# Two zero regions of dv: copied from memory by GpSimd in transfers of 4, 2, 2 and 8 rows, with one zero store issued earlier

## The chip, the cores and the metric

The kernel runs on one core of one Trainium2 chip. The metric is the device time in microseconds (us), from start to end of the program. Before the change its median over three runs is 283.13 us (282.75 to 283.57). The profiled execution took 283.0 us, of which the profile shows a span of 281.0 us; all times of events below are counted from the start of that span.

A core has five engines with instruction streams of their own: PE (matrix products), DVE and ACT (elementwise work and moving results out of the accumulators), POOL or GpSimd, and SP or SyncE, which computes nothing and here issues nearly all transfers. Transfers between memory (DRAM) and the on-chip buffer (SBUF) are carried out by 16 DMA engines, and a transfer of 128 rows is dealt out over all of them. GpSimd and ACT can issue transfers too, through queues of their own, onto the same 16 engines.

## The reference

The reference is one decoding step of a small transformer block and the gradients of all its inputs. Four sequences, one new token each, width 512. Attention has 32 query heads on 8 key/value heads of size 128, over a cache of 4096 positions of which only the last W = 1024 are used:

```python
W = min(4096, max(256, Sk // 4))                                # 1024 of 4096
q = (x @ wq).reshape(B, Sq, Hq, Dh).transpose(0, 2, 1, 3)
k = jnp.repeat(k_cache[:, :, Sk - W:, :], rep, axis=1)
v = jnp.repeat(v_cache[:, :, Sk - W:, :], rep, axis=1)
p = softmax(einsum("bhqd,bhkd->bhqk", q, k) * Dh ** -0.5)
A = einsum("bhqk,bhkd->bhqd", p, v).transpose(0, 2, 1, 3).reshape(B, Sq, Hq * Dh) @ wo
ffn = (gelu(xn @ w_gate) * (xn @ w_up)) @ w_down                # xn = layernorm(x), x of A
out = x + A(xn) + ffn(xn)
outputs: out, d x, d k_cache, d v_cache, d wq, d wo, d w_gate, d w_up, d w_down
```

What matters here: the gradients of the two caches have the caches' full shape, (4, 8, 4096, 128) in bf16, 33.6 MB each. Only the last 1024 positions of each head hold computed values. The first K0 = 3072 positions are zero and have to be written all the same: 25 MB in each, 50 MB in all, of the 81 MB that the kernel writes.

## The kernel before

Outputs are called out_0 to out_8; out_2 is dk, out_3 is dv, out_4 the gradient of wq (dwq), out_5 that of wo (dwo), out_6 to out_8 those of the feed-forward weights.

First comes the feed-forward part (lines 552 to 715), then a loop over NT = 4 groups t of two key/value heads each (lines 725 to 753). In a group the scores are formed from the keys, softmax follows, the same with the values, and then the gradients. Work that can wait (the products for dv, dk, dwo and dwq, and moving them to staging tiles) is put into a queue of small pieces, `bg`, and `tick(n)` takes n pieces from it between the steps of the main work. So the pieces for dwo, dk and dwq of group t are done during group t+1, and those of the last group at the end (line 754).

Every finished staging tile is stored by SyncE through `store` (line 100), which sets out that output stores write disjoint parts and need not wait for each other. Stores of computed data are of kind "rest", those of zeros of kind "zeros".

The zeros come from one SBUF tile, `ztile` (128 rows of 6144 bf16 values, 12,288 bytes each), cleared by GpSimd at the start (line 167). The list `zlist` (line 159) holds 32 regions: for each sequence b and each pair of heads g, one of out_2 and one of out_3, in turn. `zero(n)` (line 161) takes the next n regions from its front and stores each with one SyncE transfer of 1.5 MB: 128 rows of 12,288 bytes, eight for each DMA engine.

Where the zero stores stand is written out by hand: three at the start, one behind some of the feed-forward stores, one behind every dv and dk store (line 490), a few by themselves in the first group, four in the last group after the steps on the values (`zero(4)`, line 734), and whatever is left at the end (line 755). SyncE issues in program order, so a zero store also stands ahead of all stores that follow it. By the end two regions are left, the last two of sequence 3.

GpSimd issues six loads of weights (`load_w`, line 120). Its last instruction in group 3 is the product o_s inside `odq(t, 0)` (line 463); after that it has nothing to do. The change touches `zero`'s list, `piece_q` (the dwq pieces, line 513, with the store at line 524), and the main loop.

## Time and profile before

| what | before |
|---|---|
| time, median of 3 | 283.13 us |
| span of the profile | 281.0 us |
| PE, DVE, ACT, POOL busy | 72%, 58%, 42%, 14% of the span |
| moved by DMA | 112.12 MB, mean 399 GB/s |
| read from, written to memory | 30.68 MB, 81.01 MB |
| queue of SyncE | 103.56 MB, 89.6% of the 16 engines' span |
| queue of GpSimd | 6.29 MB, 5.6% |
| last SyncE stores issued | 263.25 us (two zero stores) |
| zero stores | 32 of 1536 KB, median 18.1 us from issue to landing |

In the windows and the page, "DMA share" is the mean busy share of the 16 DMA engines: 1.00 is all of them, 0.06 is one. Its value can be a little over 1, since packets overlap at their ends. A transfer "lands" engine by engine: each of the 16 engines reports its own share as done, and the transfer is complete when the last has reported. An issue on SyncE (SPq in the views) is the instruction that starts a transfer; the transfer itself runs later, behind those already queued.

### The profile page before, as it was taken

How to read it: one execution, taken by the hardware profiler on the slowest of the kernel's cores; microseconds unless marked ns; L12 is line 12 of the kernel's file. 1: busy time of each engine (PE TensorE's matmuls, PEld its weight loads, DVE VectorE, ACT ScalarE, POOL GpSimd, SP SyncE). 2: the span in 40 equal slices, each digit the busy share in tenths (PEclk: the TensorE clock that was granted, in tenths of full speed). 3: DMA queues.
4: the chain of work that ended last, by engine and by line, in shares of the span. 5: the costliest groups of instructions: out<-in, count | busy, mean ns of one | idle time of the engine just before them, and what ended most of it. 6: DMA issues, size and time to landing. Idle time of an engine off the chain costs nothing.

```text
span 281.0 us, 6867 instructions
## 1 busy us (share of the span) xinstructions
PE 203.1 (72%) x2972; PEld 138.8 (49%) x2972; DVE 164.1 (58%) x313; ACT 117.8 (42%) x219; POOL 40.1 (14%) x40
## 2 busy tenths in 40 slices
PE   0276699959789889998999299898999599390000
PEld 0265476735456665566775156677556484140000
DVE  7946646645776655577666067767677728386000
ACT  2030386635035418764448056443866038370000
POOL 8600000007002150002250000223000400000000
PEclk9999589986999999999999969999999979977555
DMA  7999999999999999999999999999999999999990
GB/s 264 393 375 431 431 426 417 425 419 424 369 395 424 422 420 420 426 415 422 419 417 411 412 424 423 431 383 398 385 368 415 387 432 410 425 429 422 398 422 30
DMA packets 19565, 112.12 MB, mean 399 GB/s; under 512 B 1664, under 2 KB 4496, under 8 KB 11088
## 3 DMA queue, kind: packets, MB, share of 16 engines
q1 hardware_dynamic: 17744, 103.56, 89.6%
q0 software_dynamic: 1632, 6.29, 5.6%
q10 hardware_dynamic: 160, 1.84, 1.9%
q8 instruction: 23, 0.38, 0.5%
q14 instruction: 6, 0.05, 0.0%
HBM read 30.68 MB, written 81.01 MB: 397 GB/s over the span
## 4 chain that ended last, share of the span: by engine, by line
PE 47%; DMA 22%; DVE 16%; ACT 4%; issue 2%; SPq 0%; DVEq 0%; ACTq 0%
DMA out_dram<-stg_dv 13%; PE T_ps L279 8%; PE kv_ps L484 7%; DMA wd_sb<-in_B_w_down_dram 6%; PE S_ps L345 5%; PE od_ps L450 5%; DMA out_dram<-osb_g 4%; DVE T_sb L98 3%; DVE dS_s L367 2%; PE wdT_ps L279 2%; PE dwq_ps L520 2%; PE acc_ps L256 2%; PE dwd_ps L660 2%; DVE P_s L367 2%; PE wgT_ps L279 2%
## 5 line engine op out<-in xcount | busy, mean ns | idle before, releaser
L98 DVE COPY T_sb<-T_ps 128x1024 bf16<-128x1024 bf16 x64 | 44.1, 688 | 26.7 <-PE T_ps L279 26.5
L97 ACT CAST stg_dk<-kv_ps 128x512 bf16<-128x512 f32 x52 | 29.2, 588 | 31.2 <-PE kv_ps L484 12.4
L97 ACT CAST stg_dv<-kv_ps 128x512 bf16<-128x512 f32 x51 | 28.1, 588 | 24.9 <-PE kv_ps L484 24.3
L484 PE MATMUL kv_ps<-qmr,dS_s 128*128 128x512 bf16 x64 | 23.9, 414 | 11.3 <-ACT stg_dk L97 10.6
L463 POOL TENSOR_TENSOR o_s<-od_r,msk_r 128x512 bf16<-128x512 bf16 x8 | 9.1, 1157 | 110.2 <-DVE od_r L455 80.9
L484 PE MATMUL kv_ps<-domr,P_s 128*128 128x512 bf16 x64 | 21.3, 382 | 0.0
L279 PE MATMUL T_ps<-ident,vb 128*128 128x128 bf16 x256 | 20.3, 225 | 0.4 <-DVE T_sb L98 0.4
L279 PE MATMUL T_ps<-ident,kb 128*128 128x128 bf16 x256 | 20.4, 225 | 0.0
L279 PEld LDWEIGHTS <-kb 128*128 128x128 bf16 x256 | 17.5, 101 | 4.5 <-issue 1.3
L279 PEld LDWEIGHTS <-vb 128*128 128x128 bf16 x256 | 17.2, 101 | 5.0 <-issue 3.2
L97 ACT CAST osb_q<-dwq_ps 128x512 bf16<-128x512 f32 x25 | 14.6, 587 | 8.3 <-PE dwq_ps L520 7.4
L329 POOL TENSOR_TENSOR domr<-r,msk 128x1024 bf16<-128x1024 bf16 x4 | 7.6, 1892 | 71.2 <-DVE r L326 65.1
L97 ACT CAST osb_g<-dwg_ps 128x512 bf16<-128x512 f32 (+1 forms) x25 | 12.3, 544 | 12.3 <-PE dwg_ps L673 6.3
L97 ACT CAST osb_o<-dwo_ps 128x512 bf16<-128x512 f32 x24 | 13.9, 586 | 4.5 <-PE dwo_ps L505 2.9
L98 DVE CAST stg_dk<-kv_ps 128x512 bf16<-128x512 f32 x12 | 8.0, 688 | 12.0 <-DMA out_dram<-stg_dv 11.2
L98 DVE COPY wgT<-wgT_ps 128x1024 bf16<-128x1024 bf16 x14 | 9.6, 686 | 6.8 <-PE wgT_ps L279 6.8
L345 PE MATMUL S_ps<-T_sb,qm 128*32 128x256 bf16 x128 | 12.7, 387 | 0.6 <-DVE T_sb L98 0.5
L345 PE MATMUL S_ps<-T_sb,dom 128*32 128x256 bf16 x128 | 12.7, 388 | 0.1
L505 PE MATMUL dwo_ps<-dyr,o_s 128*128 128x512 bf16 x32 | 12.4, 413 | 0.3 <-ACT stg_dk L97 0.2
L98 DVE COPY woT<-woT_ps 128x1024 bf16<-128x1024 bf16 x16 | 11.0, 686 | 2.7 <-PE woT_ps L279 2.3
L484 PEld LDWEIGHTS <-dS_s 128*128 128x128 bf16 x64 | 6.2, 101 | 12.2 <-issue 11.1
L520 PE MATMUL dwq_ps<-od_r,xnm 128*128 128x256 bf16 x64 | 11.6, 274 | 0.3 <-ACT osb_q L97 0.2
(188 smaller groups left out, 385.0 us busy)
## 6 DMA issues: line engine op xcount, KB each, us to landing
out_dram<-ztile SPq DMA_DIRECT2D x32, 1536.0 KB, 18.1
kb<-in_A_k_cache_dram SPq DMA_DIRECT2D x8, 1024.0 KB, 17.4
vb<-in_A_v_cache_dram SPq DMA_DIRECT2D x8, 1024.0 KB, 20.7
out_dram<-stg_dv SPq DMA_DIRECT2D x8, 1024.0 KB, 13.0
out_dram<-stg_dk SPq DMA_DIRECT2D x8, 1024.0 KB, 20.8
out_dram<-osb_o SPq DMA_DIRECT2D x8, 512.0 KB, 17.4
out_dram<-osb_q SPq DMA_DIRECT2D x8, 512.0 KB, 13.8
out_dram<-osb_g SPq DMA_DIRECT2D x8, 448.0 KB, 14.3
```

The source lines that it names most:

```text
L97: return nc.scalar.copy(out=out, in_=in_)
L98: return nc.vector.tensor_copy(out=out, in_=in_)
L256: nc.tensor.matmul(ps[:, c, :], lhsT=lf(c), rhs=rhs, start=(k == 0), stop=(k == len(terms) - 1))
L279: nc.tensor.transpose(ps[:, i, :], a, ident[:])
L329: nc.gpsimd.tensor_tensor(out=mr[:].rearrange("p g q d -> p (g q) d"), in0=r4[:, k, :].unsqueeze(1).broadcast_to([P, SL, Dh]), in1=msk[:]. ...
L345: nc.tensor.matmul(ps[b * RB:(b + 1) * RB, :], lhsT=zt[:, b * GP + g, c0:c0 + RB], rhs=T_sb[:].rearrange("p (x b) -> p b x", b=B)[:, b, :] ...
L367: nc.vector.scalar_tensor_tensor(out=out[:], in0=src[:].unsqueeze(2).broadcast_to([P, WQ, B]), scalar=rr[:, 0:1], in1=mskb[:].unsqueeze(1) ...
L450: nc.tensor.matmul(od_ps[g * 32:g * 32 + B * rep, k, g, :], lhsT=cols[:, jj, g * NQ + q, :], rhs=blks[(t, g)][:, j, :], start=(j == 0), st ...
L463: nc.gpsimd.tensor_tensor(out=o_s[:, g], in0=rows[:, g].unsqueeze(1).broadcast_to([P, rep, Dh]), in1=msk_r[:].unsqueeze(2).broadcast_to([P ...
L484: nc.tensor.matmul(mps[:].rearrange("p q d -> p (q d)"), lhsT=src[:, j * P:(j + 1) * P], rhs=mr[:, g].rearrange("p q d -> p (q d)"), start ...
L505: nc.tensor.matmul(mps[:], lhsT=o_s[:, g].rearrange("p r d -> p (r d)")[:, i:rep * Dh:rep], rhs=dyr[:], start=True, stop=True)
L520: nc.tensor.matmul(mps[:, i].rearrange("p g d -> p (g d)"), lhsT=xnm[:, i2 * 2 + i, c * P:(c + 1) * P], rhs=dq_r[:].rearrange("p g d -> p ...
```

## The change

Three edits:

1. A function `zero_14` takes the last two out_3 regions (sequence 3, heads 4 to 7, one block of four heads x 3072 positions) out of `zlist`. The first 14/16 of each head's positions are written by three GpSimd transfers of 4, 2 and 8 rows (a row is 192 positions of each of the four heads), which copy zeros from out_2[0], where they have been stored long before. Between the first and the second of these stands a short transfer of two rows of 4 KB from `ztile`. It writes 32 positions of one head. The last 2/16 of each head, less those 32 positions, are left to four SyncE stores from `ztile`, of 16 rows each, that are returned as a list and issued at the very end.
2. `zero_14` is called in the last group after `odq(t, 0)`, that is, behind the product o_s on GpSimd.
3. One zero store is issued earlier, behind the last dwq store of group 1 (the second group); and the last group's `zero(4)` becomes `zero(2)`. With the two regions gone, one full zero store is left for the end, followed by the four small ones.

The purpose of 1 is to let a part of the zeros be written by chosen DMA engines rather than by all 16 alike: 4 + 2 + 8 rows go to fourteen of them[...]. All zeros are still written, each once.

```diff
+    def zero_14():
+        last = [z for z in zlist if z[0] is out_3][-2:]
+        for z in last:
+            zlist.remove(z)
+        b, g = last[0][1:]
+        assert last[1][1:] == (b, g + ZR)
+        dst = out_3[b, g:g + 2 * ZR]
+        NH, KR = 4, K0 // 16
+        k0 = 14 * KR
+
+        def rest(eng, n, h, k0, w):
+            src = ztile[0:8 * n - 7:8] if n < 16 else ztile[0:n]
+            store(eng, dst[h, k0:k0 + n * w, :].rearrange("(m j) d -> m (j d)", m=n), src[:, 0:w * Dh], "zeros")
+
+        r0 = 0
+        for n in (4, 0, 2, 8):
+            if not n:
+                rest(nc.gpsimd, 2, 0, k0, 16)
+                continue
+            s_, d_ = (x[0:NH, r0 * KR:(r0 + n) * KR, :].rearrange("g (m j) d -> m g (j d)", m=n) for x in (out_2[0], dst))
+            store(nc.gpsimd, d_, s_, "zeros")
+            r0 += n
+        assert r0 * KR == k0
+        return [lambda h=h: rest(nc.sync, P, h, 0, K0 // P) for h in range(NH, 2 * ZR)] + [
+            lambda h=h, u=u: rest(nc.sync, 16, h, k0 + u, (K0 - k0 - u) // 16) for h, u in enumerate([32] + [0] * (NH - 1))]
...
             if k == 3:
                 store(nc.sync, out_4[...], held["osb"][...], "rest")
+                zero(t == NT - 3 and c2 == ND // 2 - 1)
...
             if t == NT - 1:
-                zero(4)
+                zero(2)
             link(len(chain))
             softmax_d(t)
             link()
             odq(t, 0)
+            if t == NT - 1:
+                rest = zero_14()
             load_kv(t + 2, 1)
...
         tick(len(bg))
         zero(len(zlist))
+        for z in rest:
+            z()
```

## The prediction

> **What bounds the kernel now.** I read the page's row of DMA load first, then its list of transfers, then the windows of the last 120 us, then SyncE's issues in order of time, and last the landing records in the trace (one for each of the 16 DMA engines' share of a transfer).

> The page's DMA rows, 40 slices of 7.03 us each:

> ```profile
> DMA  7999999999999999999999999999999999999990
> GB/s 264 393 375 431 431 426 417 425 419 424 369 395 424 422 420 420 426 415 422 419 417 411 412 424 423 431 383 398 385 368 415 387 432 410 425 429 422 398 422 30
> ...
> out_dram<-ztile SPq DMA_DIRECT2D x32, 1536.0 KB, 18.1
> ```

> The transfers fill the span, and 32 zero stores of 1.5 MB are 50 of its 112 MB. Only the last slice is empty: 30 GB/s. The windows (us, busy us of PE, PEld, DVE, ACT, POOL, granted clock, DMA share, GB/s) say who still works there:

> ```profile
> 180.00:195.00 15.00, 13.12 (x252) 9.91 (x251) 11.63 (x25) 7.01 (x14) 5.49 (x4) 1.00 0.97 397
> 195.00:222.00 27.00, 25.29 (x337) 15.93 (x334) 18.48 (x35) 15.77 (x29) 0.77 (x1) 1.00 0.94 385
> 222.00:240.00 18.00, 15.39 (x200) 10.00 (x201) 11.10 (x21) 9.45 (x18) 2.25 (x2) 0.91 1.02 423
> 240.00:260.00 20.00, 7.84 (x37) 3.57 (x35) 12.06 (x21) 6.11 (x12) 0.00 (x0) 0.81 1.01 422
> 260.00:274.00 14.00, 0.00 (x0) 0.00 (x0) 0.00 (x0) 0.00 (x0) 0.00 (x0) 0.50 1.00 412
> 274.00:276.00 2.00, 0.00 (x0) 0.00 (x0) 0.00 (x0) 0.00 (x0) 0.00 (x0) 0.50 0.15 61
> 276.00:280.00 4.00, 0.00 (x0) 0.00 (x0) 0.00 (x0) 0.00 (x0) 0.00 (x0) 0.50 0.05 22
> ```

> After 260 no compute engine works, so computing does not set the end. From 274 to 276 a share of 0.15 is 2.4 engines of 16, and after 276 about one (0.06 would be one): a single DMA engine works alone for some 4 us. The landings agree: the last zero store's sixteen shares land at 274.4 (first), 274.5 (median), 275.5 (fifteenth) and 279.94 (last). The same gap of 5.3 to 6.1 us between median and last stands behind every store from 213 on. It had reached 6 us by 110 and then moved between 3.4 and 8.4. So one engine is about 6 us late, and the end is its end.

> ```profile
> 216.54 3.15 SPq L103 DMA_DIRECT2D out_dram<-osb_q  x2
> 219.74 4.40 SPq L103 DMA_DIRECT2D out_dram<-ztile  x4
> 233.63 0.54 SPq L103 DMA_DIRECT2D out_dram<-stg_dv  x1
> ...
> 259.52 1.72 SPq L103 DMA_DIRECT2D out_dram<-osb_q  x2
> 263.25 1.98 SPq L103 DMA_DIRECT2D out_dram<-ztile  x2
> ```

> These issues (start, us taken) wait for older transfers: eight completion semaphores go round, and a transfer waits for the one eight before it, its slowest share included. In 195 to 222 that and the sparse output leave the other engines 6% idle (27 x 0.06 = 1.6 us). The late engine never is: its shares land 3.8 to 4.1 us apart per zero store there, and 3.66 is the pure time.

> [...] The trace of before has only GpSimd transfers of 128 rows[...]. [...] the trace shows GpSimd's loads landing while SyncE's stores run. [...] No memory-to-memory transfer is in the trace of before, so none of this settles the rate.

> **The change part by part.**

> *Removed from the even stream: two zero stores.* Each gives every engine 8 rows of 12,288 B; the median landings of the burst at 219.74 are 3.66 us apart. Two are 7.3 us on each of the 16 engines, the late one too.

> *Added: the copies.* On 14 engines, one row from each of four heads: 4 x 192 positions x 256 B = 196,608 B, just what two zero stores gave. At the stores' rate that is 7.3 us again[...]. I take the stores' rate. For it: packets of loads (memory is read) and of stores (memory is written) take the same time by size (8,192 B in 0.31 us, 12,288 B in 0.46)[...]. [...]

> *The skipped two engines* get 4 KB from the short transfer and their part of the rest.

> *The rest, four SyncE stores at the end*: 384 positions x 256 B a head = 98,304 B, over 16 rows 6,144 B an engine, four times 24.6 KB = 0.92 us at 12,288 B in 0.457. The skipped pair so has 0.92 + 0.15 = 1.07 us in place of 7.3: relieved by 6.2 us. The other 14 have 0.92 us more.

> *Issue on GpSimd.* Its last work before is the o_s product, done at 224.3; nothing is queued behind it but the closing drain. A GpSimd transfer of 1,024 rows took 1.06 us to issue (at 67.6); these have a few rows each, under 1 us. The added wait, on the zeros of out_2[0] that they read, is for stores landed by 45 us: free. Their 7.3 us an engine have from 224 to 274 to fit in.

> *Moved: one zero store behind the osb_q stores at 177.5.* It costs an engine 3.66 us there and saves it at 219.74, where two zeros now stand instead of four. For the late engine, always busy, that is nothing. For the others it can fill up to the 1.6 us idle after 195. The chain of compute ends at 258, some 20 us before the end, so outputs queued a little later behind it are hidden.

> *Sum.* Late engine: 279.94 - 6.2 = 273.7. Others: median 274.5 + 0.92 = 275.4, the second latest 275.5 + 0.92 = 276.4, less 0 to 1.6 of filled idle. I take 0.5 of that: last landing 275.9, and the end is 4.0 us earlier: 283.1 - 4.0 = 279.1.

> **The rivals.**

> *A: a late engine relieved, copies at the stores' rate*: 279.1, with 277.2 if all idle time is filled and the second latest is the other skipped engine (last landing 274.0).

> *B: copies at half rate.* The 14 engines get 7.3 us more: 276.4 + 7.3, less 0 to 1.6 and less 1 if the second latest is skipped, is 281.1 to 283.7 against 279.94: slower by 1.2 to 3.8, about 285.5. [...] against it that packet times depend on size alone.

> *C: the wrong pair.* The profile names no engine[...]. If the late engine is among the fourteen, it gets 0.92 us more: 284.0. For it: nothing in the profile says that the late engine holds the third pair of places. Against: it has been late for over 150 us and in steady measure, so it is a lasting trait that a fixed choice can meet.

> *D: in between.* If a copied byte costs half as much again (3.7 us), the others end near 279.6: no change.

> *E: copies one behind the other.* If each waits for the one before, three times 7.3 us, shared with the stores' queue, is some 44 us after 224: 268, still hidden. Only with a much smaller share of the engine's turns would they pass 275; the end would be 290 or later.

> **How the numbers follow.** A 0.58, B 0.21, C 0.11, D 0.07, E 0.03. Faster takes A and a sliver of D: 0.60; same 0.07; slower B, C, E: 0.33. Predicted is A, 279.1. The range goes from A's best, 277.0, up to B's middle and a little beyond, 286.0: below it and above it lie half of B's upper part, E and C with slow copies, under 2 in 10.

> **What would show it.** Right: the last windows drop from a full share to nothing within 2 us, with no engine alone for 4 us; the late engine's last landing is near or before the median; the copies' packets take as long per byte as the stores'; the share in 195 to 222 nears 1. Wrong: copy packets at half the stores' rate, with 14 engines ending together and two idle (B); one engine still alone at the end, 1 us later (C); GpSimd transfers issued one by one, tens of us apart (E). If the gap comes from the run and not from the engine, and wanders, the choice of engines means nothing.

## The result and the profile after

The changed kernel takes 284.75 us (median of 4 runs, 283.97 to 285.25), the kernel before 283.08 in the same comparison. The ratio is 1.0055, with a 95% interval of 1.0028 to 1.0082: the change makes the kernel slower, by 1.7 us between the medians. The profiled execution of the changed kernel was the fastest of its four (283.97 us); its span is 282.3 us, against 281.0 before.

The DMA rows of the page of the changed kernel (40 slices of 7.06 us), the queue of GpSimd and the bytes moved:

```profile
DMA  7999999999999999999999999999999998999990
GB/s 273 387 375 431 429 427 419 417 417 418 357 389 427 415 417 425 424 420 423 416 409 409 419 428 424 425 417 424 423 421 419 412 415 354 415 425 424 398 301 20
...
q0 software_dynamic: 1904, 9.05, 8.1%
...
HBM read 33.43 MB, written 81.01 MB: 405 GB/s over the span
```

As many bytes are written as before, and 2.75 MB more are read: the zeros that now come from memory. The last slice is as empty as it was (20 GB/s), and the one ahead of it has dropped from 422 to 301. That slice's busy share is still a 9, so the engines are at work there and move less (from 272 to 274, below, a share of 0.96 goes with 194 GB/s): it holds the four small stores, whose packets turn out to be slow (0.650 us in the mean, against 0.234 at the late engine; see the part on why the prediction was wrong). The windows of the last part (us, then busy us of PE, PEld, DVE, ACT, POOL, granted clock, DMA share, GB/s):

```profile
195.00:222.00 27.00, 24.90 (x322) 15.54 (x318) 18.86 (x35) 15.78 (x29) 1.14 (x2) 1.00 1.01 419
222.00:240.00 18.00, 15.77 (x201) 10.17 (x202) 11.03 (x22) 9.60 (x19) 4.13 (x5) 0.91 0.98 392
...
260.00:270.00 10.00, 0.00 (x0) 0.00 (x0) 2.13 (x5) 0.00 (x0) 0.00 (x0) 0.61 0.99 405
...
272.00:274.00 2.00, 0.00 (x0) 0.00 (x0) 0.00 (x0) 0.00 (x0) 0.00 (x0) 0.50 0.96 194
274.00:276.00 2.00, 0.00 (x0) 0.00 (x0) 0.00 (x0) 0.00 (x0) 0.00 (x0) 0.50 0.48 98
276.00:280.00 4.00, 0.00 (x0) 0.00 (x0) 0.00 (x0) 0.00 (x0) 0.00 (x0) 0.50 0.06 26
280.00:282.00 2.00, 0.00 (x0) 0.00 (x0) 0.00 (x0) 0.00 (x0) 0.00 (x0) 0.50 0.01 3
```

From 195 to 222 the share has gone from 0.94 to 1.01: the moved zero store does fill the idle time. But from 276 to 280 the share is still that of one engine, as before, and a little of it now reaches past 280. DVE still has five instructions after 260, where before it had none: computing ends some us later, but with a share of 0.99 the DMA engines never run dry there.

SyncE's issues in order of time (start, us taken). The moved zero store stands at 179.20, two zero stores stand where four stood, and the last burst holds one zero store and the four small ones:

```profile
179.20 0.66 SPq L103 DMA_DIRECT2D out_dram<-ztile  x1
...
219.37 2.77 SPq L103 DMA_DIRECT2D out_dram<-ztile  x2
...
266.17 6.59 SPq L103 DMA_DIRECT2D out_dram<-ztile  x5
```

GpSimd's instructions in order of time. The four transfers follow the product o_s at once, without a wait for the zeros that they read:

```profile
220.86 3.02 POOL L491 TENSOR_TENSOR o_s<-od_r,msk_r 128x512 bf16<-128x512 bf16 x2 [29.34 <-DVE cc L461]
223.82 0.63 POOL L103 DMA_DIRECT2D out_dram<-out_dram  x1
224.45 0.56 POOL L103 DMA_DIRECT2D out_dram<-ztile  x1
224.98 1.15 POOL L103 DMA_DIRECT2D out_dram<-out_dram  x2
```

The list of transfers gives the median us from issue to landing in the last column:

```profile
out_dram<-out_dram POOLq DMA_DIRECT2D x1, 1536.0 KB, 18.2
...
out_dram<-out_dram POOLq DMA_DIRECT2D x1, 768.0 KB, 15.0
out_dram<-out_dram POOLq DMA_DIRECT2D x1, 384.0 KB, 17.2
...
out_dram<-ztile POOLq DMA_DIRECT2D x1, 8.0 KB, 15.1
```

Issue and landing together put the last of them at about 244, far ahead of the end. The copies are not what comes last. That leaves the landings of the last store's sixteen shares, from the records in the trace:

```
us                first    median   fifteenth  last
before            274.4    274.5    275.5      279.94
changed           274.96   275.69   275.84     280.77
```

One share still lands about 5 us behind the median. The late engine was not relieved; it got later by 0.83 us.

### The profile page after: what moved, and what is told of

Same layout as the page of the kernel before. It is cut to its first block, busy times and chain, and to the rows that moved or that the text cites. A ratio compares the mean times of both kernels' runs of the same rounds, so it can differ in the third digit from the quotient of the medians.

```text
span 282.3 us, 6874 instructions
## 1 busy us (share of the span) xinstructions
PE 204.2 (72%) x2972; PEld 139.7 (49%) x2972; DVE 164.2 (58%) x313; ACT 118.1 (42%) x219; POOL 42.5 (15%) x44
## 4 chain that ended last, share of the span: by engine, by line
PE 32%; DMA 21%; issue 20%; DVE 12%; POOL 5%; ACT 3%; DVEq 0%; ACTq 0%; POOLq 0%
DMA out_dram<-stg_dv 14%; DMA wq_sb<-in_A_wq_dram 7%; PE kv_ps L512 6%; PE T_ps L307 5%; PE od_ps L478 5%; PE S_ps L373 4%; PE dwq_ps L548 3%; DVE dS_s L395 2%; DVE T_sb L98 2%; POOL ztile L195 2%; PE dwo_ps L533 2%; DVE wqT L98 2%; PE pT_ps L307 2%; PE acc_ps L284 1%; DVE P_s L395 1%
## 5 line engine op out<-in xcount | busy, mean ns | idle before, releaser
L548 PE MATMUL dwq_ps<-od_r,xnm 128*128 128x256 bf16 x64 | 12.5, 299 | 0.1
## 6 DMA issues: line engine op xcount, KB each, us to landing
out_dram<-ztile SPq DMA_DIRECT2D x30, 1536.0 KB, 19.3
```

Source lines behind the costliest of these rows:

```text
L548: nc.tensor.matmul(mps[:, i].rearrange("p g d -> p (g d)"), lhsT=xnm[:, i2 * 2 + i, c * P:(c + 1) * P], rhs=dq_r[:].rearrange("p g d -> p ...
```

## The experiments

**Which engine does what: how it was read.** The records of single packets do not name their engine, but on an engine that has work one packet starts as the one before it ends (the late engine's last seven zero packets in the kernel before take 0.460 us each and start 0.457 apart), so they can be chained, end to start. In the changed kernel the late engine's chain is known by its packets of osb_q (the staging tile of dwq), 2,048 bytes each: after about 230 it is the only one that still has them. It also carries small marks. A GpSimd transfer leaves, on each engine that gets no row of it, as many 4-byte packets as a row has pieces (4 for a copied row, 1 for the short transfer's), and on every engine one packet that reports its share. In the changed kernel this adds up: 4 x 16 reports + 4 x 12 + 1 x 14 + 4 x 14 + 4 x 8 = 214 (transfers of 4, short, 2 and 8 rows), and 214 four-byte packets of that queue are there after 200 us. So the number of marks ahead of the late engine's own copies, and behind them, tells which transfer gave it a row.

In the changed kernel there are 7 ahead and 6 behind. Seven is 4 + 1 for the 4-row copy and 1 + 1 for the short one, and six is its own report and 4 + 1 for the 8-row copy: the late engine has a row of the 2-row copy, right behind the short transfer. Its four copied pieces take 2.01, 1.95, 2.01 and 1.87 us, 7.8 us in all, and between one piece and the next stands one packet of osb_q, 0.08 to 0.11 us (at 231.47, 233.50 and 235.59).

Two theories fit that. Both suppose what no trace of before shows, that the rows of GpSimd's copies are given to the 16 engines in turn, in the order of issue; how far the runs agree stands in the part on why the prediction was wrong. A place is a position in that order, counted from 0. *Shifted engine*: the short transfer takes two places as the prediction had it, and the late engine sits at places 6 and 7 of the order. *No place*: the short transfer takes no place at all; the 2-row copy falls on places 4 and 5, and it is the last two places that go free. The runs below vary the order and what the short transfer is. In each list, "short" stands for the short transfer (0 in the code).

**The short transfer first.** Edit of the changed kernel:

```diff
-        for n in (4, 0, 2, 8):
+        for n in (0, 2, 4, 8):
```

> Order short, 2, 4, 8: the first pair of places is skipped instead of the third. If the late engine is of the first pair: 279 to 280, last landing within 2 us of the median. If it is of the second pair: as the changed kernel, 284.7, one engine 5 us late. If the engine wanders from run to run: between, with a wide interval.

284.87 us, 1.0069 [1.0043, 1.0095]. Marks 7 ahead, 6 behind. Ahead are the short one (2) and the 2-row copy (5), behind are its own report and the 8-row copy: a row of the 4-row copy.

**The short transfer second.**

```diff
-        for n in (4, 0, 2, 8):
+        for n in (2, 0, 4, 8):
```

> Order 2, short, 4, 8: the second pair of places is skipped. If the late engine is of the second pair: 279 to 280, last landing within 2 us of the median. If it is of the first pair: 284.7. If the engine wanders from run to run: between, with a wide interval. If the copies cost more than their bytes, neither order comes below 282.

284.73 us, 1.0056 [1.0036, 1.0075]. Marks 7 and 6: again the 4-row copy. These two and the changed kernel bear both theories: places 6 and 7 with a short transfer that counts, or places 4 and 5 with one that does not.

**All in pairs.** Eight copies of two rows, all 16 rows, so that no engine is spared and no rest is left:

```diff
-        k0 = 14 * KR
+        k0 = 16 * KR
...
-        for n in (4, 0, 2, 8):
+        for n in (2,) * 8:
...
-        return [lambda h=h: ...
+        return []
```

> All sixteen rows are copied, by eight GpSimd transfers of two rows, so every pair of engines has a transfer of its own and no engine is skipped. Fixed late engine, missed by the choice of places: seven of the transfers land within about 2 us of each other and one lands 5 to 8 us after them; its place in the order is the place of the late engine, and I expect the first or second pair (in the changed kernel the four landings of the 4-row transfer include the engine whose store landed 13 us late). Lateness that comes from the copies themselves: all eight land alike. Time 283 to 284 either way.

283.91 us in the one execution there is, beside 283.36 for the kernel before. Here every engine gets by copy what two zero stores gave it, and the time is 0.5 us longer, so copying is no great burden in itself, as far as one execution tells. The late engine has 9 marks ahead and 26 behind. Behind, 26 = 1 + 5 x 5: five pairs follow its own, which makes its own the third of eight, places 4 and 5, and not the first or second that I expected. Ahead, 10 were to be expected and one record is missing. With nothing but copies in the list, this count does not depend on what the short transfer does. It speaks against the shifted engine. I missed that at first and took the three runs above for places 6 and 7.

**The move alone.** Edit 3 stays, edits 1 and 2 are out; the two regions stay in the list:

```diff
-                rest = zero_14()
+                rest = []
```

> Only the earlier zero store and two instead of four zero stores in the last group; no copies, all 32 regions stored by SyncE. Theory that the late engine alone sets the end: it is never idle, so 283.1 within 0.5, with the DMA share of 195 to 222 raised from 0.94 to about 1. Rival that the move itself costs time: 284 or more.

283.36 us, 0.9998 [0.9989, 1.0006]: no difference. The windows show why:

```profile
195.00:222.00 27.00, 24.63 (x311) 15.26 (x308) 19.14 (x35) 15.76 (x29) 1.42 (x2) 1.00 1.00 418
222.00:240.00 18.00, 15.97 (x203) 10.08 (x204) 11.15 (x22) 10.08 (x19) 1.60 (x1) 0.91 0.84 348
...
276.00:280.00 4.00, 0.00 (x0) 0.00 (x0) 0.00 (x0) 0.00 (x0) 0.00 (x0) 0.50 0.05 22
```

The idle time of 195 to 222 is filled and comes back as a share of 0.84 from 222 to 240, and the end is the one late engine's, whose last share lands at 279.98 (before: 279.94).

**The short transfer for places 6 and 7.** If the engine sits there and the short transfer counts, this order relieves it:

```diff
-        for n in (4, 0, 2, 8):
+        for n in (4, 2, 0, 8):
```

> Order 4, 2, short, 8. In three runs the late engine's packets (the only ones of 2,048 bytes after 230 us) are followed by six 4-byte packets of GpSimd's queue after its copies, which fits only places 6 and 7: behind the 2-row transfer of the changed kernel, within the 4-row transfer of the two others. Fixed late engine: with places 6 and 7 skipped its last landing comes within 1.5 us of the median, the others end near 276.0, and the time is 279.3 (278.5 to 280.3). Rival, copies slow the whole stream: not below 282.

284.44 us, 1.0039 [1.0026, 1.0053]. A miss. The marks are 5 ahead and 8 behind: 5 is the 4-row copy alone, 8 is its own report, the short one (2) and the 8-row copy (5). The late engine is in the 2-row copy once more, now at places 4 and 5 however one counts. The shifted engine has fallen: a short transfer that took places would have put the 2-row copy of the changed kernel at 6 and 7, and the late engine has a row of it in both kernels.

The short transfer's own packets say the same. There are two of 4,096 bytes, so it does run on two engines. In the changed kernel they start at 238.30 and 238.77, each on an engine whose four copied pieces came without a mark ahead and were followed at once by the report: engines of the 4-row copy, not the two next in the round. In the order 4, 2, short, 8 one of the two can be followed, and it is again on an engine of the 4-row copy; in the order 2, short, 4, 8 it is on an engine of the first 2-row copy. So these rows stay with engines of the first copy wherever the short transfer stands in the order.

The same without the moved zero store, and the same with two heads in place of four in the copies, were to share out the gain that this order did not bring.

```diff
-                zero(t == NT - 3 and c2 == ND // 2 - 1)
...
-                zero(2)
+                zero(4)
```

> Places 6 and 7 skipped, but the zero store isn't moved and the last group keeps four zero stores, so no full one is left for the end. The others' idle time of 195 to 222 then stays unfilled: 1 to 1.6 us above the version with the move, near 280.6. Rival, the move does nothing once the late engine is relieved: the same as with it.

```diff
-        NH, KR = 4, K0 // 16
+        NH, KR = 2, K0 // 16
```

> Only two of the four heads copied past places 6 and 7, the other two stored evenly by SyncE. The relief is halved to 3.1 us: the late engine lands near 276.9 and sets the end again, 0.5 to 1 us above the others: time 280.0. Rival, time is not set by the late engine: no difference from four heads.

284.58 us, 1.0040 [1.0025, 1.0056], and 284.71 us, 1.0038 [1.0023, 1.0053]. Both are missed for the same reason: the engine was not relieved, so neither says anything on its question. In both, the late engine has its row of the 2-row copy (marks 4 ahead, one fewer than the count asks for, and 8 behind; with two pieces a row, 3 and 6).

**Is it GpSimd's loads that make the engine late?** In the kernel before, the late engine's lag grows from 4.6 us at its landing at 145.97 to 8.4 at 154.75, while two of these loads run (issued at 142.46 and 144.77, landed at 155.80 and 163.85). That they cause it is not shown. The kernel before, with its six weight loads issued by SyncE, has no GpSimd transfer at all:

```diff
-    def load_w(t, eng=nc.gpsimd):
+    def load_w(t, eng=nc.sync):
```

> The kernel before with its six weight loads issued by SyncE instead of GpSimd; nothing is copied. If GpSimd's loads are what makes one engine late (its lag grew by 2 and by 4 us while they ran, at 105 to 112 and 147 to 155): the lag behind the median after 150 us is under 3 us, and the time falls to 279 to 281. If the engine is slow whoever issues: lag of 5 to 7 us as before and 283.3 or a little more.

284.43 us, 1.0041 [1.0026, 1.0057]. The last windows:

```profile
276.00:280.00 4.00, 0.00 (x0) 0.00 (x0) 0.00 (x0) 0.00 (x0) 0.00 (x0) 0.50 0.06 28
280.00:282.00 2.00, 0.00 (x0) 0.00 (x0) 0.00 (x0) 0.00 (x0) 0.00 (x0) 0.50 0.03 12
```

One engine is still alone at the end, and the time is about 1 us longer than before. The last zero store has its median at 274.09 and its last landing at 281.69, a lag of 7.6 us against 5.4 before. So it does not take GpSimd's loads: with no transfer of GpSimd, an engine is as late or later. That it is the same engine is not shown, since only copies of GpSimd tell its place.

**A short transfer that takes a place.** If *no place* is right, what differs is the kind of transfer: the copies, from memory to memory, take their places in turn, and the short one, from rows of SBUF, does not. So the short one becomes a copy too: 16 positions of each of four heads in two rows, 8,192 bytes for an engine. The order stays 4, short, 2, 8.

```diff
-                rest(nc.gpsimd, 2, 0, k0, 16)
+                s_, d_ = (x[0:NH, k0:k0 + 16, :].rearrange("g (m j) d -> m g (j d)", m=2) for x in (out_2[0], dst))
+                store(nc.gpsimd, d_, s_, "zeros")
...
-            lambda h=h, u=u: rest(...) for h, u in enumerate([32] + [0] * (NH - 1))]
+            lambda h=h, u=u: rest(...) for h, u in enumerate([16] * NH)]
```

> Order 4, short, 2, 8 as in the change, but the short transfer is a memory-to-memory copy of two rows (of four heads, 8 positions each) instead of two rows of SBUF. In all kernels with copies the 4-byte packets of the late engine fit one reading: it holds the third pair of places, and the short transfer from SBUF takes no place, so that the 2-row copy behind it falls on that pair and the last pair goes free instead. Then a short copy from memory takes the third pair: the late engine is relieved by 6.2 us, nobody is alone at the end, 279.3 (278.5 to 280.5). Rival, the late engine wanders or the short transfer's source is no matter: 284.5 as before.

279.71 us, 0.9857 [0.9830, 0.9885], beside 283.60: faster than the kernel before by 3.9 us, and faster than the changed one. The page's DMA rows, and the windows:

```profile
DMA  7999999999999999999999999999999999999995
GB/s 269 389 373 433 429 429 413 422 421 419 346 387 424 373 406 393 425 418 431 419 408 404 425 417 430 420 417 425 422 426 422 396 426 405 386 424 428 429 418 148
```

```profile
195.00:222.00 27.00, 25.56 (x338) 16.17 (x339) 18.29 (x35) 15.75 (x29) 0.03 (x1) 1.00 1.01 420
...
272.00:274.00 2.00, 0.00 (x0) 0.00 (x0) 0.00 (x0) 0.00 (x0) 0.00 (x0) 0.50 1.00 326
274.00:276.00 2.00, 0.00 (x0) 0.00 (x0) 0.00 (x0) 0.00 (x0) 0.00 (x0) 0.50 0.54 106
276.00:280.00 4.00, 0.00 (x0) 0.00 (x0) 0.00 (x0) 0.00 (x0) 0.00 (x0) 0.50 0.01 4
```

The slice ahead of the last is full (418 GB/s), the last one holds 148 in place of 20, and after 276 there is next to nothing: no engine works alone for 4 us. The last store lands at 275.75 (median), 276.86 (fifteenth) and 277.14 (last).

The relief can be followed in the records. Ahead of the copies one engine is as late as ever: an osb_q store lands at 225.27 (median) and 233.16 (last), a lag of 7.9 us. Between that engine's osb_q packets of 2,048 bytes stand the two packets of one row of the short copy (4,096 bytes each, at 230.14 and 230.42), and no piece of 49,152. So the late engine has a row of the short copy, as meant. Behind the copies its lag is gone: the sixteen shares of a dv store issued at about 234 all land between 240.1 and 244.2, with the last 1.3 us behind the median. One share is now 2 to 3 us ahead of all others up to the end (272.45 for the last store); I take it for the other engine of the spared pair, which had nothing to make good.

**The control.** The same copy as the short transfer, put where places 6 and 7 go free:

```diff
-        for n in (4, 0, 2, 8):
+        for n in (4, 2, 0, 8):
```

(on top of the edit above)

> The same short copy from memory, but in the order 4, 2, short, 8: places 6 and 7 are skipped. Fixed late engine in the third pair: not relieved, 284.5, one engine 5 us late. Rival, any change of the short transfer helps: 279.3 here too.

284.84 us, 1.0049 [1.0032, 1.0066].

```profile
276.00:280.00 4.00, 0.00 (x0) 0.00 (x0) 0.00 (x0) 0.00 (x0) 0.00 (x0) 0.50 0.08 32
280.00:282.00 2.00, 0.00 (x0) 0.00 (x0) 0.00 (x0) 0.00 (x0) 0.00 (x0) 0.50 0.04 18
```

The same transfers in another order cost 5.1 us, and the engine at the end is back; its last share lands at 281.87. Its chain has pieces of 49,152 bytes, its own report and then the marks of the short copy: a row of the 2-row copy. So it is the choice of the pair, and not the memory copy, that makes the gain.

**The move, once the engine is relieved.**

```diff
-                zero(t == NT - 3 and c2 == ND // 2 - 1)
...
-                zero(2)
+                zero(4)
```

(on top of the memory copy, order 4, short, 2, 8)

> Short copy from memory in the change's order, without the earlier zero store and with four zero stores in the last group. The others' idle time of 195 to 222 stays unfilled, 1 to 1.6 us: 280.5. Rival, the move is nothing: 279.3.

282.14 us, 0.9951 [0.9931, 0.9971].

```profile
195.00:222.00 27.00, 25.60 (x338) 16.20 (x339) 18.30 (x35) 15.76 (x29) 0.00 (x0) 1.00 0.93 377
...
274.00:276.00 2.00, 0.00 (x0) 0.00 (x0) 0.00 (x0) 0.00 (x0) 0.00 (x0) 0.50 0.96 347
276.00:280.00 4.00, 0.00 (x0) 0.00 (x0) 0.00 (x0) 0.00 (x0) 0.00 (x0) 0.50 0.40 86
```

The move is worth 282.14 - 279.71 = 2.4 us here, more than the 1 to 1.6 expected, and nothing alone. The idle time is read off directly: 27 x (1.01 - 0.93) = 2.2 us from 195 to 222. Without the move nearly all engines work on to 276 (share 0.96), and some beyond. Idle time of the fifteen counts only when they set the end.

**How much to copy.** Three heads in place of four (on top of the memory copy):

```diff
-        NH, KR = 4, K0 // 16
+        NH, KR = 3, K0 // 16
```

> Short copy from memory, change's order, but three heads copied and the fourth stored evenly by SyncE. Relief of the late engine 4.7 us in place of 6.2, and 0.7 us instead of 0.9 more for the others: both ends meet near 276, 279.2, the same as with four heads. Rival, the late engine is later than the others by more than 5 us at this point (its lag before the copies was 7.6 in the changed kernel): it sets the end again, 280.5.

279.93 us, 0.9857 [0.9828, 0.9887]: the same as with four. The last store lands at 275.0 (median) and 275.77 (last) in the profiled execution, the fastest of the four (278.94 us), so the engines are still more even there, but the median time does not show it.

## Why the prediction was wrong

**The end is one late engine's end.** Right. Every kernel in which that engine was not relieved ends as before or later; the one order that relieves it brings 3.9 us.

**"The skipped two engines" get the short transfer.** This step failed. I counted all four transfers as places in one round, which no trace of before shows. For the copies the runs agree with that as far as the late engine tells: counted in the order of issue, its row is the fifth or sixth copied row in seven of the nine kernels whose packets were counted, and one of the third to sixth in the other two (those of the 4-row copy behind a 2-row one). The short transfer from two SBUF rows takes no place. Its rows went to two engines of the 4-row copy (at 238.30 and 238.77). The 2-row copy behind it so falls on the third pair, where the late engine is: it got 7.8 us of copies where it was to be spared. The two engines that go free are the last pair, which had nothing to make good. They show in the trace of the changed kernel: of the dv store issued at 233.30, two shares land at 238.24 and 238.27, ahead of the other fourteen (240.6 to 248.8). That lead is not kept. From 238 to 239 the DMA share is 0.87, which is about two engines of 16 without work; at the next store (issued at 233.88) the two are 1.3 us ahead (242.97 and 243.01, the third 244.29), and by 255 a single us. What holds them up at 238 is not shown. One free engine's chain can be followed: 17 marks (5 + 2 + 5 + 5) and no row. That the free pair is the last in that order follows from the count, and was not seen by itself.

The short transfer's rows keep to engines of the first copy in the three orders where they could be followed. Why is not shown; what the runs show is that a memory copy in the same place counts (279.71 us, the late engine relieved) and the SBUF rows do not (284.75 us).

**The late engine "relieved by 6.2 us".** It did not happen, as a consequence. It got its 7.3 us by copy (7.8 as measured), like the others, and 0.92 us of the rest on top: rival C's sum. Its last landing was to be 0.92 later and was 0.83 later. The remainder of the 1.2 us in the span is the closing: from the last landing to the end of the span 1.09 us before, 1.50 after, in GpSimd's closing instructions (from its clearing of the semaphores to the end of the drain behind it 0.08 us before, 0.59 after). I had not counted that term. It is there in the faster kernel as well (278.60 - 277.14 = 1.46). The number of GpSimd transfers does not set it: with eight of them, in the kernel with all in pairs, it is 1.22.

**Against rival C I had put that a lasting trait can be met by a fixed choice.** That was true and no argument. The late engine's place fits the same third pair in all nine kernels with copies whose packets were counted, one profiled execution each (the experiments on chips 5, 6 and 12), and a fixed choice does meet it (279.71 us). Whether this fixed choice met it was the open question, and nothing in the profile of before could answer it. With one open premise under a chance of 0.58, 0.11 for C was too little. (B, C and E add up to 0.35, not to the 0.33 put down for slower; that changes nothing.)

**The copies' rate.** Right: 49,152 bytes took 1.815 us at the median (27.1 GB/s an engine) and 1.95 in the mean, and the zero stores' 12,288 bytes take 0.460 at the median there, 26.7 GB/s. In the mean the four pieces are 7.8 us, against 7.3 worked out. So half the rate (B) and half as much again (D) fell. One behind the other (E) fell too: the four transfers are issued within 2.3 us and have all landed 15 to 18 us after their issue, at the same time as SyncE's stores.

**Issue under 1 us each, the added wait free.** Right: 0.63, 0.56 and 1.15 us for two, directly behind o_s.

**The move fills idle time, "I take 0.5 of that".** The mechanism was right and the size too small: with the late engine relieved it is worth 2.4 us.

**The rest, "four times 24.6 KB = 0.92 us".** Right for the late engine, and too small for the others. The packets of the four small stores in the changed kernel, from the records (one of 5,632 or 6,144 bytes for an engine and store):

```
                                    us
late engine, 279.43 to 280.35       0.215, 0.234, 0.234, 0.234
others, 271.8 to 275.5              0.22 to 0.95, 27 of 60 over 0.9
mean of all 64                      0.650
```

Alone, the late engine writes its four in 0.92 us, just the sum in the prediction. The others write theirs at the same time, and then nearly half of the packets take about 0.93 us, four times the 0.234: four times 0.65 is 2.6 us an engine in place of 0.92. I had priced a packet by its size alone, as most other packets in these traces may be priced (12,288 bytes: median 0.460 us, mean 0.468). It costs nothing here, where the late engine ends 5 us later. In the kernel with the memory copy the mean is 0.47, or 1.9 us for four, and there it is on the path.

**The sum.** With the right pair the working holds in size: a gain of 4.0 us was the sum, and the kernel with the memory copy gains 3.9. That it is so near is in part luck, for terms off in both directions cancel: the move gave 1.9 more than I took; the small stores took 1.0 more, the copies 0.6 (four of 1.98) and the closing 0.4.

**Open.** What makes the one engine slow is not settled. An engine is as late without GpSimd's loads, and where copies tell its place it is in the same pair of GpSimd's order on three chips; which of the pair it is was not shown. Nor is it settled why the small stores slow each other. They write sixteen rows side by side in memory, and they also read sixteen rows side by side of `ztile`; no run changes one without the other. What lengthens the closing is open too.

## What to carry to other kernels

When a saturated stream of stores sets the end, look at the landings of the last store engine by engine. Here the slowest engine's last share came at 279.94 of a span of 281.03 us, 4.4 us behind the fifteenth, and only work taken from that engine was gained, until another came last. A scheme that chooses engines rests on how transfers are dealt out, so first run it with transfers of one kind, and read from the packets which engine got what. A part of a change that is worth nothing alone (the move: 283.36 us in the experiment, and 283.36 for the kernel before) may be worth microseconds once another bound is gone (2.4 here), so measure it on top of the mended version too.

## What the runs showed of the hardware

The closing of the program behind the last landing took 1.09 us before, 1.50 in the changed kernel with four GpSimd transfers at its end, and 1.22 with eight.

One engine of 16 landed its last share 3.2 to 7.6 us behind the median at the end of every kernel here that did not relieve it. In the changed kernel its lag was 7.6 us ahead of its copies, 15.5 right behind them, and 5.1 at the end.

Zero packets of 6,144 bytes, one for an engine and store, took 0.234 us with one engine at work and in nearly half of the cases about 0.93 with the other fifteen at work on such stores.
